# Another order for the first loads and a re-made issue list in a one-core SSM convolution and gated feed-forward kernel

## The chip, the cores and the metric

The kernel runs on one core of a Trainium2 chip. The metric is the device time of one execution in microseconds (us), as the median of several runs. Before the change it is 196.39 us (three runs, 195.62 to 196.74).

## What is computed

The reference, cut to what matters (S = 2048 rows, D = 512, feed-forward width 1792, all bf16):

```python
xn = layernorm(A_q)
# A: shift convolution (4 taps) of k, times v, then a long convolution over the 2048 rows
k_shift = sum_t k_pad[t:t+S] * shift_k[:, ks-1-t]
kv = k_shift * v
y  = irfft(rfft(kv_pad) * rfft(ssm_k_pad))[:S] + kv * ssm_D
s  = xn * y
# B: gated feed-forward
g  = silu((gelu_tanh(xn @ w_gate) * (xn @ w_up)) @ w_down)
out = A_q + s * g
```

## The kernel before

**The work.** The feed-forward runs in four quarters q of 512 rows. For each quarter `ln(q)` (L821 to L835) normalizes four row tiles of 128 (statistics and scaling on VectorE, DVE; the power on GpSimd, POOL), and the tiles are turned with the feature on the partitions: quarters 0 and 1 by transposes on TensorE (PE, L854) and copies into `xnT`, quarters 2 and 3 by a DMA. `unit(q, m)` makes slice m of 14 (128 of the 1792 columns): a gate product and an up product on PE, four matmuls of 512 columns each; ScalarE (ACT) puts the gate through a gelu into `GE` (L1137); DVE multiplies the up product by it into `HT` (L1140). Slices 0 and 1 of quarter 0 are made in two halves of 256 columns (L1128, L1130), the first half from row tiles 0 and 1, the second from tiles 2 and 3. `down(q)` multiplies `HT` by `Wd`. The weights `Wg` and `Wu` come in four pieces each: piece 0 for slices 0 and 1, piece 1 for slices 2 to 5, piece 2 for 6 to 9, piece 3 for 10 to 13.

The long convolution is a Fourier transform in two stages through three scratch tensors in HBM (`ZH`, `ZK`, `ZI`). The filter `ssm_k` arrives as four pieces `Hn` 0 to 3. Pieces 0 and 1 are turned on PE (L878) and evicted as `HTr`. Pieces 2 and 3 are reordered on ACT into `HP` (four copies called HP below, 128x1024 elements, through `copy`, L609: two from piece 2, two from piece 3) and turned by two DMA transposes into `HTD` (L899). `stage1_h` multiplies `HTr` (tasks H) and `HTD` (tasks J) by the Fourier matrix `F1` on PE, ACT evicts, a DMA stores to `ZH`; the J tasks share four buffers, each free again when its store has landed. `stage1_k` does the same for k times v (tasks K). `h_stage2`, `spectrum` and the loop over `psy` do the second stage, the product and the inverse.

**What sets the order.** Nothing is ordered by the loops. `Sched.add` collects some 790 tasks; the string `SEQ` lists them by number, and `Sched.run` goes through `SEQ` in that order, gives each task an engine and takes a buffer or PSUM bank for it by a cost model of its own; then all tasks are emitted in that order. So each engine's instructions stand in the order of `SEQ` and run strictly in it, and a product waits until the earlier user of its PSUM bank, fixed by the list, has been evicted. The costs in the model only choose buffers and banks; the waits are real semaphores. An HP copy stands in the model with `act(1024, True)`, a gelu of 512 columns with `act(512)`; `act(n, sb)` is 170 + 0.833 n, and 30 more for a source in SBUF, in ns.

`ORDER` numbers the input loads; they are issued by SyncE (SP) in the order of `SEQ`, and the DMA transposes and the stores of J and K stand in the same SP queue. A DMA transpose that waits holds up all that stands behind it on SP. The transposes `MI` (two) and `G1` (L1039) share one semaphore, so each waits until the one before has landed. `LANDS` are the model's landing times of the first loads, in ns.

Eleven warm-up matmuls (L618 on a zero tile) stand first on PE. The last thing on PE is the last tile of `down(3)`, followed by silu on ACT (L1172), two DVE steps (L1174, L1175) and the store.

Of the kernel before, what the change touches and what calls it, by code (L numbers as in the profile page):

```python
# [22 lines left out]
LAST = [(0, 384), (384, 512)]  # L23
TURN = 8192
N_WARM = 11
ORDER = "x01 h0 x11 h1 x22 w0 w1 h2 h3 D0 w2 s0 k0 v0 x1 w3 k1 v1 d0 d1 k2 v2 k3 v3 x2 x3"
SEQ = (
# [22 lines left out]
)  # L50
NF_BANKS = 4
ISSUE = 470.0
# [239 lines left out]
class Sched:  # L292
# [8 lines left out]
    FIRST = {"loads": 1050.0, "SP": 30500.0}  # L301
    DRAIN = 121.0
    EARLY, TAKEN, SHARED, WAIT = (0.0, 1.0), 1400.0, 46000.0, 3300.0
    LANDS = (3150.0, 3490.0, 5770.0)

    def __init__(self):
        self.tasks = []
# [37 lines left out]
    def run(self):  # L345
# [5 lines left out]
        for name in SEQ.split():  # L351
# [13 lines left out]
            if eng == "loads":  # L365
                free[eng] = t.start + dur * (self.EARLY[1] if t.start < self.EARLY[0] else 1.0)
                if n_loads < len(self.LANDS):
                    free[eng] = self.LANDS[n_loads] - self.LOAD_LAT
                n_loads += 1
# [29 lines left out]
def build_kernel(nc, A_q, A_k, A_v, A_shift_k, A_ssm_k, A_ssm_D, B_w_gate, B_w_up, B_w_down, out):  # L399
    with ExitStack() as es0:  # L400
# [408 lines left out]

        for what in ORDER.split():  # L810
            if what[0] in "xa" and len(what) == 3:
# [475 lines left out]
```

## Time and profile before

| | |
|---|---|
| median of the runs shown | 196.39 us |
| time of the profiled execution | 195.77 us |
| its span | 194.0 us |
| PE busy in the span | 187.5 us (97%) |
| DVE / ACT / POOL busy | 159.8 / 125.5 / 14.0 us |
| DMA traffic | 49.19 MB, mean 254 GB/s |
| clock granted to PE | full in all slices |

Times in the profile count from the start of the span; the profiled execution took 1.77 us more than its span. A line of the timeline has start, duration, engine, source line, operation, output and inputs, count, and in brackets the idle time before it with what ended it. "x4" merges four instructions; the matmuls are pipelined, so four take less than four times one. SPq and ACTq are DMA issues; "us to landing" runs from the issue to the semaphore.

### The profile page before, as it was taken

Reading aid. Unit: us, or ns where it says so; the run is one execution under the profiler, and the core shown is the slowest. Engines: PE = TensorE matmul, PEld = TensorE weight load, DVE = VectorE, ACT = ScalarE, POOL = GpSimd, SP = SyncE. Lnnn points to the kernel's source line nnn. Section 1 sums busy time; section 2 is a strip of 40 time slices with the busy share of each in tenths; the row PEclk is TensorE's granted clock in tenths of the full one; section 3 lists DMA queues with packets and bytes.
Section 4 is the critical chain, followed back from the end, with each engine's and each line's share of the span. In section 5 each row is a group of like instructions: output and inputs, shape, how many; then the busy total and the mean of one; then the engine's idle time right before and its main releaser. Section 6 shows DMA issues by size and latency. Waiting matters only on the chain.

```text
span 194.0 us, 3492 instructions
## 1 busy us (share of the span) xinstructions
PE 187.5 (97%) x1364; PEld 85.0 (44%) x1377; DVE 159.8 (82%) x245; ACT 125.5 (65%) x170; POOL 14.0 (7%) x32
## 2 busy tenths in 40 slices
PE   7799999999998999999999999999999999999993
PEld 2594544444443444443434433433444434444442
DVE  7599699998999993977788789878897963588993
ACT  6787999979876978868648767756577531222121
POOL 6412420000000000020300000000000000000000
PEclk9999999999999999999999999999999999999999
DMA  5999999999999859999999991893714344939333
GB/s 165 327 322 349 377 403 315 188 217 375 368 363 355 242 210 231 384 345 283 277 306 221 318 312 41 291 332 106 237 37 184 105 150 135 402 109 363 126 139 135
DMA packets 46102, 49.19 MB, mean 254 GB/s; under 512 B 12803, under 2 KB 39943, under 8 KB 46086
## 3 DMA queue, kind: packets, MB, share of 16 engines
q1 hardware_dynamic: 37510, 42.67, 69.8%
q10 hardware_dynamic: 8576, 6.29, 10.1%
q8 instruction: 11, 0.18, 0.4%
q14 instruction: 5, 0.04, 0.1%
HBM read 27.39 MB, written 14.68 MB: 217 GB/s over the span
## 4 chain that ended last, share of the span: by engine, by line
PE 87%; DMA 7%; ACT 2%; issue 1%; SPq 1%; DVE 1%
PE psall L618 80%; PE psall L1028 5%; DMA Hn<-in_A_ssm_k_dram 3%; DMA ZH<-X 3%; SPq L590 1%; PE psall L854 1%; ACT G L609 1%; PE psall L878 1%; ACT X L609 1%; ACT ASX L609 0%; ACT GE L1137 0%; DVE G L1175 0%; DVE G L1174 0%; ACT G L1172 0%
## 5 line engine op out<-in xcount | busy, mean ns | idle before, releaser
L618 PE MATMUL psall<-xnT,Wu 128*128 128x512 bf16 (+1 forms) x232 | 55.8, 372 | 0.0
L618 PE MATMUL psall<-xnT,Wg 128*128 128x512 bf16 (+1 forms) x232 | 55.3, 372 | 0.0
L618 PE MATMUL psall<-Wd,HT 128*128 128x512 bf16 (+2 forms) x231 | 50.8, 366 | 0.7 <-issue 0.5
L1140 DVE TENSOR_TENSOR HT<-psall,GE 128x512 bf16<-128x512 f32 x54 | 36.7, 685 | 15.2 <-PE psall L618 13.6
L1137 ACT ACTIVATE GE<-psall 128x512 bf16<-128x512 f32 x54 | 31.7, 601 | 12.6 <-PE psall L618 12.2
L618 PEld LDWEIGHTS psall<-Wd,HT 128*128 128x128 bf16 x238 | 22.4, 98 | 25.9 <-issue 1.1
L618 PEld LDWEIGHTS psall<-xnT,Wu 128*128 128x128 bf16 x232 | 21.6, 98 | 25.9 <-issue 3.8
L618 PEld LDWEIGHTS psall<-xnT,Wg 128*128 128x128 bf16 x232 | 21.9, 98 | 25.3 <-issue 1.3
L609 ACT ACTIVATE X<-psall 128x1024 bf16<-128x1024 f32 (+1 forms) x18 | 15.1, 846 | 3.8 <-DMA ZH<-X 3.3
L609 ACT ACTIVATE HS<-psall 128x1024 bf16<-128x1024 f32 x14 | 13.7, 1022 | 4.2 <-PE psall L1028 4.2
L1164 ACT ACTIVATE G<-psall 128x512 bf16<-128x512 f32 x12 | 7.0, 597 | 12.8 <-PE psall L618 12.4
L1011 DVE TENSOR_TENSOR KAC<-KAC,KTM 128x2048 bf16<-128x2048 bf16 x12 | 14.6, 1218 | 0.1
L1009 DVE TENSOR_TENSOR KTM<-KK,SKB 128x2048 bf16<-128x2048 bf16 x12 | 14.6, 1217 | 0.0
L609 ACT ACTIVATE BO<-psall 128x1024 bf16<-128x1024 f32 x9 | 9.1, 1023 | 8.2 <-PE psall L1028 7.7
L821 DVE BATCH_NORM_STATS2 stats<-X 128x6 f32<-128x512 bf16 x16 | 10.3, 677 | 3.9 <-DMA X<-in_A_q_dram 3.9
L609 ACT ACTIVATE KB<-psall 128x1024 bf16<-128x1024 f32 x11 | 11.0, 1021 | 3.6 <-PE psall L1028 3.6
L609 ACT ACTIVATE AST<-psall 128x1024 bf16<-128x1024 f32 x12 | 12.3, 1031 | 1.2 <-PE psall L618 1.0
L612 DVE CAST BO<-psall 128x1024 bf16<-128x1024 f32 x7 | 8.5, 1223 | 3.7 <-PE psall L1028 3.7
L1172 ACT ACTIVATE G<-psall 128x512 bf16<-128x512 f32 (+2 forms) x5 | 2.6, 512 | 13.1 <-PE psall L618 13.1
L1091 DVE TENSOR_TENSOR HW<-KB,HW 128x1024 bf16<-128x1024 bf16 x16 | 10.9, 682 | 0.0
L1091 DVE TENSOR_TENSOR HS<-KB,HS 128x1024 bf16<-128x1024 bf16 x16 | 10.8, 682 | 0.0
L618 PE MATMUL psall<-V,F 128*128 128x512 bf16 x30 | 8.8, 379 | 0.4 <-ACT ASX L609 0.3
(83 smaller groups left out, 172.2 us busy)
## 6 DMA issues: line engine op xcount, KB each, us to landing
BH<-ZH SPq DMA_DIRECT2D x8, 512.0 KB, 6.3
HW<-HS SPq DMA_DIRECT2D x16, 256.0 KB, 2.9
BK<-ZK SPq DMA_DIRECT2D x8, 512.0 KB, 5.1
ZI<-BO ACTq DMA_DIRECT2D x16, 256.0 KB, 2.9
BI<-ZI SPq DMA_DIRECT2D x8, 512.0 KB, 4.1
ZK<-AST SPq DMA_DIRECT2D x6, 512.0 KB, 3.7
Hn<-in_A_ssm_k_dram SPq DMA_DIRECT2D x4, 512.0 KB, 8.4
KK<-in_A_k_dram SPq DMA_DIRECT2D x4, 512.0 KB, 8.8
```

The lines of the kernel that those rows point to most:

```text
L609: return h.activation(o, i, ACTF.Copy, scale=scale)
L612: return h.tensor_copy(o, i)
L618: return h.matmul(o, lhsT=l, rhs=r, start=st, stop=sp)
L821: t_stats[t] = op([("DVE", 670.0)], lambda e, h, t=t: h.bn_stats(stats[:, t, :], X[:, t, :]), r=[bX[q][t % 4]], w=[bst[t]], rr=[R_X[t]], w ...
L1009: op([("DVE", dur)], lambda e, h, j=j, m=m: h.tensor_tensor(KTM[:, m.slot, :, :], kk(j), sk(j), ALU.mult), r=need + [bSKB[j], a], w=[m], r ...
L1011: op([("DVE", dur)], lambda e, h, m=m: h.tensor_tensor(KAC[:, a.slot, :, :], KAC[:, a.slot, :, :], KTM[:, m.slot, :, :], ALU.add), r=[m], ...
L1028: trk.op("PE", lambda h: h.matmul(ps(s, i)[b, :], lhsT=wt(col)[a, :], rhs=data(col)[a, :], start=n < 16, stop=n >= len(todo) - 16, tile_po ...
L1091: return hd.tensor_tensor(o, flat(KB, kb[h]), o, ALU.mult)
L1137: op([("ACT", act(512))], lambda e, h: h.activation(GE[:, g.slot, :], bank(pg), ACTF.Gelu_apprx_tanh), r=[pg], w=[g], rr=lambda: R_bank(pg ...
L1140: op([("DVE", dve(512, 1))], lambda e, h: h.tensor_tensor(HT[:, q % 2, m, :], bank(pu), GE[:, g.slot, :], ALU.mult), r=[pu, g], w=[bHT[q][m]],
L1164: op([("ACT", act(n))], lambda e, h, g=g, pc=pc: h.activation(g, pc(), ACTF.Tanh, scale=0.5), r=[p], w=[bt], rr=lambda p=p: R_bank(p), ww= ...
L1172: op([("ACT", act(n))], lambda e, h, g=g, pc=pc: h.activation(g, pc(), ACTF.Silu), r=[p], w=[bt], rr=lambda p=p: R_bank(p), ww=rg, after=z ...
```

## The change

```diff
-ORDER = "x01 h0 x11 h1 x22 w0 w1 h2 h3 D0 w2 s0 k0 v0 x1 w3 k1 v1 d0 d1 k2 v2 k3 v3 x2 x3"
+ORDER = "x02 h0 h1 x22 w0 w1 h2 h3 D0 w2 s0 k0 v0 x1 w3 k1 v1 d0 d1 k2 v2 k3 v3 x2 x3"
 SEQ = (
-    "17 19 18 0 3 1 2 4 8 5 7 11 21 6 9 51 12 66 67 68 74 20 69 76 75 50 10 77 13 53 22 83 23 84 87 118 70 108 71 72 113 55 73 88 78 79 54 370 52 "
+    "0 1 3 17 18 5 11 7 8 9 19 4 2 12 67 50 49 68 6 10 20 65 66 13 75 76 52b 83 73 117 74 87b 118 112 82 86 113 53 102 54 21 369 69 22 70 56 77 "
...
-    LANDS = (3150.0, 3490.0, 5770.0)
+    LANDS = (4350.0, 5700.0, 7000.0, 8420.0, 9400.0, 10250.0)
```

All of `SEQ` differs in its text, since the first row load is one task now and later numbers shift by one. Read by tasks, the following differs.

The loads on SP (KB): before, row tile 0 (128), tile 1 (128), Hn 0 (512), tiles 2 and 3 (256), Hn 1 (512), Wg and Wu piece 0 (256 each), rows of quarter 1 (512), Wg 1 (512), first rows of k (336), D (1), Wu 1 (512), Hn 2, more of k (45), Wg 2, the taps SKR, one row of zeros, k 0, Wu 2, Wg 3, Wu 3, Hn 3 (512 each), then v. After: tiles 0 and 1 in one transfer (256), Hn 0, Hn 1, tiles 2 and 3, Wg 0, Wu 0, Wg 1, rows of quarter 1, Wu 1, first rows of k, SKR, Hn 2, more of k, Wg 2, k 0, Wu 2, zeros, Hn 3, Wg 3, k 1, Wu 3, D, the first HTD transpose, two pieces of v, the second HTD transpose, then the rest.

The start of PE: up to the first gate product both lists hold the same groups (turning Hn 0 and 1, row tiles 0 and 1, six small H products). After it, before: slices 0 and 1 complete (both halves), then slices 3, 5, 2, 4. After: the first halves of 0 and 1, then slices 4, 2, 3 and the ups of 2 and 3, with the second halves between them up to slices 9 and 8.

The four HP copies on ACT: before, `HP, H, gelu 3, gelu 4, H, store, gelu 7, HP, H, gelu 6, 2 xnT, gelu 8, store, gelu 9, xnT, HP, xnT, gelu 11, store, H, HP, gelu 13`. After: `gelu 0 (second half), HP, store, gelu 9, HP, store, HP, gelu 8, HP, xnT, gelu 7, xnT, 2 stores, H, gelu 13`; the third HP is the first that reads Hn 3.

PE at that place, after: gate 0 (second half), up 4, gate 9, up 0 (second half), gate 8, one H product, the transposes of a row tile, up 9, gate 7, up 8, the transposes of another tile, gate 10, up 7, gate 13, transposes, gate 12, gate 6. Gate 10 takes the bank of gate 8, gate 13 the bank of those first transposes, gate 12 that of gate 7.

In the stage of J: after, `MI` from TFB and `G1` stand on SP ahead of the rows of quarter 2 and of the first J store, where before one `MI` stands ahead of them and `G1` comes seven stores later. The rest is small moves; the last products on PE are the same.

42 rows, old and new, of the table SEQ are left out of this document.

## The prediction

> **What bounds the kernel now.** I read the page first, then the chain of waits in order of time, then PE's own waits.
>
> ```profile
> span 194.0 us, 3492 instructions
> PE 187.5 (97%) x1364; PEld 85.0 (44%) x1377; DVE 159.8 (82%) x245; ACT 125.5 (65%) x170; POOL 14.0 (7%) x32
> ```
> ```profile
> 2.59 6.77 DMA Hn<-in_A_ssm_k_dram
> ...
> 9.40 1.17 PE psall L878 x8
> ...
> 159.07 11.82 PE psall L618 x54
> ...
> 190.23 0.02 issue
> ```
> ```profile
> PE psall L878 <- DMA Hn<-in_A_ssm_k_dram: 0.8, 2, 0.6
> PE psall L618 <- ACT ASX L609: 0.3, 1, 0.3
> PE psall L618 <- ACT X L609: 0.2, 1, 0.2
> ```
>
> The chain is a load up to 9.40 us and then nearly all PE until 190.23. From 159.07 on PE makes 54 matmuls of 512 columns in 11.82 us, 0.219 each, with nothing between them; I count 256 columns as half of that and 128 as a quarter. After 9.40 PE waits for other engines only 0.3 + 0.2 us. So the change can win little: some waiting before 9.40, and these 0.5 us. It loses wherever it makes PE wait, because PE has no idle time later in which to catch up.
>
> **First part: the loads and the start of PE.** The rows of the timeline for this part and the next, in order of time, one later HP, and the landing of the first Wg piece (size, us from issue):
>
> ```profile
> 3.06 0.43 SPq L590 DMA_DIRECT2D Wg<-in_B_w_gate_dram  x1
> ...
> 6.04 1.27 PE L878 MATMUL psall<-ident,Hn 128*128 128x128 f32 x8 [0.19 <-DMA Hn<-in_A_ssm_k_dram]
> ...
> 7.99 0.69 DVE L821 BATCH_NORM_STATS2 stats<-X 128x6 f32<-128x512 bf16 x1 [1.27 <-DMA X<-in_A_q_dram]
> ...
> 10.41 0.60 PE L618 MATMUL psall<-xnT,Wg 128*128 128x256 bf16 x4
> ...
> 10.84 0.40 DVE L835 TENSOR_SCALAR XN<-X,mv 128x512 bf16<-128x512 bf16 x1
> ...
> 11.04 0.38 ACT L1128 ACTIVATE GE<-psall 128x256 bf16<-128x256 f32 x1 [0.73 <-PE psall L618]
> ...
> 19.01 2.08 ACT L609 ACTIVATE HP<-Hn 128x1024 bf16<-128x1024 bf16 x1 [0.62 <-DMA Hn<-in_A_ssm_k_dram]
> ...
> 21.00 0.57 ACT L609 ACTIVATE X<-psall 128x512 bf16<-128x512 f32 x1
> ...
> 21.48 0.58 ACT L1137 ACTIVATE GE<-psall 128x512 bf16<-128x512 f32 x1
> ...
> 21.95 0.60 ACT L1137 ACTIVATE GE<-psall 128x512 bf16<-128x512 f32 x1
> ```
> ```profile
> 30.11 2.09 ACT L609 ACTIVATE HP<-Hn 128x1024 bf16<-128x1024 bf16 x1 [0.21 <-DMA Hn<-in_A_ssm_k_dram]
> ```
> ```profile
> Wg<-in_B_w_gate_dram SPq DMA_DIRECT2D x1, 256.0 KB, 7.2
> ```
>
> *Won.* Wg 0 lands at 3.06 + 7.2 = 10.26, and PE starts the first gate product at 10.41. After, the same KB and one issue fewer (0.43 us) stand ahead of it, so it lands between 9.8 and 10.26; I take 10.0, near the middle, and start PE there. The same groups stand on PE up to this point, and Hn 1, for which PE waits now (9.40), moves ahead of tiles 2 and 3, so PE is done with them by then: 0.4 us won. Tiles 0 and 1 in one transfer come some tenths later; PE turns Hn 0 first (6.04), so it does not see that.
>
> *Given back.* Tiles 2 and 3 take the place of Hn 1, which landed at 2.59 + 6.77 = 9.36; less 0.3 for the issue saved, 9.1. From the start of their statistics to the second normalized tile it takes 10.84 + 0.40 − 7.99 = 3.25 us, so that is ready at 12.35. Transposes, the ACT copy and the handing over (about 1.0, an estimate: a gelu's 0.58, four quarter matmuls and PE's 0.2 to be seen, below) put the first product on Wg 1 at 13.4. Behind the first gate's start at 10.0 there is work of 13 matmuls of 512 columns (half of slices 0 and 1, eight transposes, six H products), 2.85 us, so PE could have been there at 12.85: 0.55 lost.
>
> *Other loads.* Hn 2 landed at 19.0 as the 4432nd KB of the list and Hn 3 at 30.1 as the 8061st (two rows wait for them): 327 KB per us. By that rate, less 0.3, Wg 1 (2560 KB) comes at 13.0, Wu 1 (3584) at 16.1, Wg 2 (5501) at 22.0, Wu 2 (6525) at 25.1; PE asks at 13.4, 16.0, 22.15 and 25.05 by the count of its products. All are on the edge, none costs over 0.1.
>
> Sum: 0.55 lost, 0.4 won, **+0.2**. The ends: −0.45 (Wg 0 at 9.8, tiles early enough not to wait) and +0.9 (Wu 1 0.7 later than the rate says).
>
> **Second part: the four HP copies.** This decides.
>
> ```profile
> L609 ACT ACTIVATE HP<-Hn x4: 2082/2084/2107, 19.0 to 34.0; 128x1024 bf16<-128x1024 bf16 x4
> ```
> ```profile
> L609 ACT ACTIVATE HS<-psall 128x1024 bf16<-128x1024 f32 x14 | 13.7, 1022 | 4.2 <-PE psall L1028 4.2
> ```
>
> An HP takes twice as long as an eviction of as many elements (1022 ns), and keeps ACT for 21.00 − 19.01 = 1.99 us; a gelu keeps it for 21.95 − 21.48 = 0.47. The list was made with 170 + 0.833 × 1024 + 30 = 1053 ns for an HP, half of that. Before, the four are spread over 19.0 to 34.0 and enough evictions lie between them. After, the second-half gelu of slice 0, HP, gelu 9, HP, HP, gelu 8, HP and an xnT copy follow each other. Counted from the end of that half's gate on PE:
>
> - ACT sees it after 0.2 (10.41 + 4 × 0.11 = 10.85, the gelu at 11.04). Gelu 0, half the data, 0.3; HP 1.99; gelu 9 0.47; HP 1.99; HP 1.99. Gelu 8 starts at 6.94 and ends, at 0.6, at 7.54.
> - PE goes through up 4, gate 9, half of up 0, gate 8, H, transposes, up 9, gate 7, up 8, transposes: 26 full, 4 half and 8 quarter matmuls, 30 × 0.219 = 6.57. Gate 10 needs the bank that gelu 8 frees: it waits **1.0**.
> - ACT's last HP starts at 7.41 and the xnT copy runs from 9.40 to 9.98. PE, after gate 10 and up 7 (8 × 0.219), stands at 9.3 and needs that bank for gate 13: it waits **0.7**.
> - From there gelu 7 and the next follow 0.5 us apart and stay ahead of PE.
>
> The third HP also needs Hn 3. By the rate it comes as the 7040th KB at 19.0 + 2608 / 327 − 0.3 = 26.7. The half's gate ends near 21.3 on PE, so ACT asks at 21.3 + 0.2 + 0.3 + 1.99 + 0.47 + 1.99 = 26.25: **+0.4**, between 0 and 1.0. Sum **+2.1**, between +1.4 and +3.0; below that only if an HP got shorter in its new place.
>
> [...]
>
> **Third part: the stage of J and K on SP.**
>
> ```profile
> 44.16 6.98 SPq L1039 DMA_TRANSPOSE MI<-TFA  x1
> ...
> 54.98 3.38 SPq L1039 DMA_TRANSPOSE MI<-TFB  x1
> ```
> ```profile
> ACT X L609 <- DMA ZH<-X: 3.3, 3, 1.5
> ```
>
> ACT waits 3.3 us for J stores now, and 0.5 of it reaches PE. After, one `MI` and `G1`, which waits for it, stand ahead of the first J store. Held up 3.38 us like the second `MI`, the store comes about when PE, 2 us later than now, needs it: 0. Held up 6.98 like the first, it is 3.6 us later and 2 to 3 of these reach PE. The v, k and Wd loads that crowd the first `MI` now go out earlier against it, so I take **0**, between −0.5 and +3.
>
> Costed at nothing: v stands behind the first HTD transpose on SP, which waits for the third HP; K wants v some 10 us later. D's late fold and DVE's new order hide behind the waits above; a DVE step that came too late would cost PE up to that step. The last products and what follows them hold the same work.
>
> **Sum.** +0.2 + 2.1 + 0 = +2.3 us. On the profiled execution, span 194.0 and 1.77 around it, 195.77, that makes 198.1; the median lies 0.62 above that execution, and on it the forecast is 196.39 + 2.3 = **198.7 us**. About 0.5% (1.0 us) is what a measurement of this kernel can tell from no change.
>
> **The rivals.**
> - *No difference.* An HP in its new place takes what HS takes; gelu 8 then ends three times 1.0 us earlier, at 4.6, before PE asks at 6.57, and the start is left: 196.39 + 0.2 = 196.6. For it: PE waits for no eviction of this kind now. Against it: four rows within 1% of 2.09. [...] With what else may soften the term, 0.17.
> - *Faster.* One mechanism: the loads land at their early end, PE starts at 9.95 and meets no wait (−0.45), and the 0.5 us of waits on J go: 195.4. It decides at gate 10: gelu 8 must end by 6.5, so an HP may take (6.5 − 1.57) / 3 = 1.6 us. It takes 2.08. 0.05.
> - *The J stores as well.* `MI` holds SP for 7 us again: 198.7 + 2.3 = 201.0. For it: the row of 6.98. Against it: fewer loads beside it. 0.20.
> - *That the change does not do what it says* is excluded for the order; that the loads land no earlier is in the first term.
>
> **How the numbers follow.** The forecast has 0.58; its own range is 196.39 − 0.45 + 1.4 = 197.3 to 196.39 + 0.9 + 3.0 = 200.3. Faster by over 0.5%: 0.05. Within 0.5%: the second case and a little of the forecast's lower edge, 0.18. Slower: 0.77. The range leaves out the faster case, half of the case without a difference and the far half of the J case's: 196.6 to 201.0.
>
> **What would show it.** Right: PE waiting about 1 and 0.7 us for a gelu and an xnT copy between 28 and 33 us; four HP of 2.08 within 11 us; the first gate near 10.0; the last PE work near 192.5. Wrong: PE without a wait from 28 to 33; an HP near 1 us; Hn 3 after 27.3; or PE waiting over 1 us behind J stores or somewhere that I took for covered.

## The result

The changed kernel takes **202.61 us** in the median (201.64 to 203.44, six runs); the kernel before, beside it, 196.77. The ratio is 1.0297, with a 95% interval from 1.0249 to 1.0345: slower by 5.8 us. The forecast of 198.7 had the direction and 2.3 us of it, and the time lies 1.6 us beyond the upper end of the range.

The page of the changed kernel's profile, the line of the span, that of the engines and the granted clock of PE in 40 slices:

```profile
span 199.8 us, 3514 instructions
PE 190.5 (95%) x1377; PEld 84.8 (42%) x1377; DVE 160.2 (80%) x245; ACT 125.7 (63%) x170; POOL 13.1 (7%) x32
...
PEclk9999999999998799999999999999999999999999
```

The span grew by 5.8 us, the busy time of PE by only 3.0, though the work is the same; the clock row is no longer full: in slices 13 and 14, that is from 60 to 70 us, it falls to 0.8 and 0.7. PE's waits, and below them the chain of waits between 45 and 65 us (start, duration, what):

```profile
PE psall L618 <- ACT G L609: 3.3, 1, 3.3
...
PE psall L618 <- ACT GE L1137: 0.9, 1, 0.9
PE psall L618 <- ACT xnT L609: 0.5, 1, 0.5
```
```profile
46.95 8.32 DMA MI<-TFB
...
55.30 1.17 SPq L1039
...
57.13 5.45 DMA ZH<-G
```

Three places can be told apart. The two waits of 0.9 and 0.5 are the two that the prediction set at gates 10 and 13. The longest, 3.3 us, is new: the chain leads back from an eviction of a J task on ACT to the landing of the first J store, from there over SP (rows of quarter 2, `G1`) to the landing of `MI`. This is that place on SP, on ACT and on PE, and then stretches of 2 us, with the busy times of the five engines and behind them the granted clock of PE (0.95 in the first):

```profile
46.95 3.52 SPq L1039 DMA_TRANSPOSE MI<-TFB  x1
55.30 1.17 SPq L1039 DMA_TRANSPOSE G<-F  x1
56.59 0.50 SPq L590 DMA_DIRECT2D X<-in_A_q_dram  x1
57.13 0.43 SPq L590 DMA_DIRECT2D ZH<-G  x1
```
```profile
62.67 1.02 ACT L609 ACTIVATE G<-psall 128x1024 bf16<-128x1024 f32 x1 [5.91 <-DMA ZH<-G]
```
```profile
63.75 1.03 PE L618 MATMUL psall<-V,F 128*128 128x512 bf16 x2 [3.35 <-ACT G L609]
65.16 1.03 PE L618 MATMUL psall<-HTD,F 128*128 128x512 bf16 x2 [0.37 <-ACT X L609]
...
70.04 2.32 PE L618 MATMUL psall<-Wd,HT 128*128 128x512 bf16 x10
```
```profile
62.00:64.00 2.00, 0.25 (x1) 0.13 (x2) 1.82 (x2) 1.33 (x2) 0.00 (x0) 0.95 1.53 305
64.00:66.00 2.00, 1.63 (x5) 0.30 (x4) 0.00 (x0) 1.10 (x2) 0.00 (x0) 0.50 0.86 152
66.00:68.00 2.00, 2.00 (x8) 0.83 (x7) 0.34 (x1) 1.77 (x3) 0.00 (x0) 0.70 1.08 391
```

SP issues `MI` until 50.47 and then nothing until 55.30: `G1` shares its semaphore and waits until `MI` has landed (46.95 + 8.32 = 55.27). Only then come the rows and the first J store, which lands at 57.13 + 5.45 = 62.58. The fifth J task that ACT evicts needs that buffer (there are four), and ACT waits 5.91 us with it; PE waits for the bank behind it, and after 3.35 us of idling it is granted half its clock (0.50 from 64 to 66 us, 0.70 over 66 to 68) until about 67 us. From the end of the wait to the ten matmuls on `Wd` it takes 70.04 − 63.75 = 6.29 us.

The four HP copies on ACT, with the gelu of gate 8 and the xnT copy that PE waited for, and the two gates:

```profile
20.56 2.08 ACT L609 ACTIVATE HP<-Hn 128x1024 bf16<-128x1024 bf16 x1
...
23.01 2.08 ACT L609 ACTIVATE HP<-Hn 128x1024 bf16<-128x1024 bf16 x1
25.23 2.08 ACT L609 ACTIVATE HP<-Hn 128x1024 bf16<-128x1024 bf16 x1 [0.15 <-DMA Hn<-in_A_ssm_k_dram]
...
27.21 0.59 ACT L1137 ACTIVATE GE<-psall 128x512 bf16<-128x512 f32 x1
...
27.69 2.08 ACT L609 ACTIVATE HP<-Hn 128x1024 bf16<-128x1024 bf16 x1
29.66 0.59 ACT L609 ACTIVATE xnT<-psall 128x512 bf16<-128x512 bf16 x1
```
```profile
27.86 1.04 PE L618 MATMUL psall<-xnT,Wg 128*128 128x512 bf16 x4 [0.90 <-ACT GE L1137]
30.31 1.04 PE L618 MATMUL psall<-xnT,Wg 128*128 128x512 bf16 x4 [0.55 <-ACT xnT L609]
```

**Theory A**, formed from these lines: about 4.7 of the 5.8 us come from `G1` waiting on SP ahead of the J stores (3.35 + 0.37 of waits, and some 1.5 of slow products, an estimate from about 3 us of them at half the clock, less the 0.5 that the kernel before waits there); the HP copies cost their 1.5 where they stand, but most of that is hidden, since PE would only wait longer at the J stores. **Rival B**: the bulk loads and `MI` itself make the stores late, whoever waits for whom. **Rival C**: the products behind the wait are slow for another cause than the idling.

### The profile page after: what moved, and what is told of

The parts are those of the page before. It is cut to its first block, busy times and chain, and to the rows that moved or that the text cites. A ratio compares the mean times of both kernels' runs of the same rounds, so it can differ in the third digit from the quotient of the medians.

```text
span 199.8 us, 3514 instructions
## 1 busy us (share of the span) xinstructions
PE 190.5 (95%) x1377; PEld 84.8 (42%) x1377; DVE 160.2 (80%) x245; ACT 125.7 (63%) x170; POOL 13.1 (7%) x32
## 3 DMA queue, kind: packets, MB, share of 16 engines
q10 hardware_dynamic: 8576, 6.29, 9.8%
## 4 chain that ended last, share of the span: by engine, by line
PE 79%; DMA 13%; ACT 2%; issue 2%; SPq 1%; DVE 1%; ACTq 0%
PE psall L618 72%; DMA Hn<-in_A_ssm_k_dram 6%; PE psall L1028 5%; DMA MI<-TFB 4%; DMA ZH<-G 3%; ACT HP L609 1%; PE psall L878 1%; SPq L590 1%; SPq L1039 1%; ACT GE L1137 1%; ACT X L609 0%; PE psall L854 0%; DVE HTr L612 0%; DVE G L1175 0%; DVE G L1174 0%
## 5 line engine op out<-in xcount | busy, mean ns | idle before, releaser
L618 PE MATMUL psall<-Wd,HT 128*128 128x512 bf16 (+2 forms) x238 | 52.9, 367 | 0.0
L1137 ACT ACTIVATE GE<-psall 128x512 bf16<-128x512 f32 x54 | 31.2, 604 | 16.1 <-PE psall L618 12.4
L618 PEld LDWEIGHTS psall<-xnT,Wu 128*128 128x128 bf16 x232 | 22.2, 99 | 25.5 <-issue 2.4
L609 ACT ACTIVATE HS<-psall 128x1024 bf16<-128x1024 f32 x13 | 12.9, 1025 | 4.3 <-PE psall L1028 4.3
L609 ACT ACTIVATE KB<-psall 128x1024 bf16<-128x1024 f32 x12 | 12.0, 1022 | 5.6 <-PE psall L1028 5.5
L609 ACT ACTIVATE X<-psall 128x512 bf16<-128x512 f32 (+1 forms) x16 | 13.0, 823 | 2.7 <-PE psall L618 2.6
L609 ACT ACTIVATE BO<-psall 128x1024 bf16<-128x1024 f32 x10 | 9.9, 1022 | 5.5 <-PE psall L1028 5.4
L618 PE MATMUL psall<-V,F 128*128 128x512 bf16 x32 | 9.8, 394 | 3.3 <-ACT G L609 3.3
L1166 DVE SCALAR_TENSOR_TENSOR G<-G,psall 128x512 bf16<-128x512 bf16 x12 | 8.0, 681 | 5.4 <-ACT G L1164 5.4
L612 DVE CAST BO<-psall 128x1024 bf16<-128x1024 f32 x6 | 7.3, 1224 | 5.8 <-PE psall L1028 5.8
```

Source lines behind the costliest of these rows:

```text
L609: return h.activation(o, i, ACTF.Copy, scale=scale)
L612: return h.tensor_copy(o, i)
L618: return h.matmul(o, lhsT=l, rhs=r, start=st, stop=sp)
L1137: op([("ACT", act(512))], lambda e, h: h.activation(GE[:, g.slot, :], bank(pg), ACTF.Gelu_apprx_tanh), r=[pg], w=[g], rr=lambda: R_bank(pg ...
L1166: op([("DVE", dve(512, 1))], lambda e, h, g=g, pc=pc: h.scalar_tensor_tensor(out=g, in0=g, scalar=1.0, in1=pc(), op0=ALU.add, op1=ALU.mult ...
```

## The experiments

Times of one row come from one chip with runs of the kernel before beside them, so rows are compared by the ratio.

| kernel | median, us | before beside it | ratio, 95% interval |
|---|---|---|---|
| the changed kernel | 202.61 | 196.77 | 1.0297 [1.0249, 1.0345] |
| G1, MI: a semaphore each | 197.76 | 195.92 | 1.009 [1.0056, 1.0124] |
| J 0 eight times | 200.9 | 195.92 | 1.0267 [1.0193, 1.034] |
| HP in address order | 203.45 | 195.92 | 1.0378 [1.031, 1.0445] |
| semaphores, HP in address order | 196.63 | 195.92 | 1.0028 [0.9992, 1.0064] |
| first loads alone | 196.69 | 196.21 | 1.0042 [1.001, 1.0074] |
| G1 alone moved | 197.0 | 196.21 | 1.0041 [1.0019, 1.0062] |
| semaphores, HP apart | 197.27 | 196.21 | 1.0059 [1.0026, 1.0093] |
| the same, MI and G1 behind | 196.78 | 196.21 | 1.0028 [1.0003, 1.0053] |
| HP in address order, J 0 thirteen times | 201.35 | 195.75 | 1.0268 [1.0224, 1.0312] |
| MI and G1 behind as above, HP on POOL | 199.5 | 195.75 | 1.0198 [1.0165, 1.023] |
| before, MI and G1 behind | 195.84 | 195.75 | 1.0009 [0.9979, 1.0038] |

### G1 no longer waits for MI

```diff
-        d_g1 = dsem("d_g1")
+        d_g1 = [dsem(f"d_g1_{i}") for i in range(3)]
-  ... transpose=True), d_g1, r=[rr], w=[ww])
+  ... transpose=True), d_g1[0 if ww is R_G1 else 1 if ww is R_MI[0] else 2], r=[rr], w=[ww])
```

> The changed kernel with one edit: the transposes G1 and MI have a semaphore each, so G1 no longer waits on SP for the landing of the MI ahead of it; the order of the list is the same. Theory A (what SP loses from 50.5 to 55.3 us behind that landing makes the J stores, ACT's eviction of J 5 and so PE late): G1 issues within 1 us of the end of MI's issue, the first J store 3.5 to 5 us earlier, ACT waits under 2.5 us for it instead of 5.9, PE's wait of 3.35 us goes or falls under 0.7, its clock stays full from 62 to 68, and the time is 198.0 us (197.4 to 199.0), 4 to 5 below the changed kernel. Rival B (the queues are full with bulk loads, and the store comes late by these whoever waits for whom): the first store still lands at 61 us or later, and the time falls by under 1 us.

SP and PE in the profile of this kernel:

```profile
47.55 3.52 SPq L1039 DMA_TRANSPOSE MI<-TFB  x1
51.11 1.26 SPq L1039 DMA_TRANSPOSE G<-F  x1
52.49 0.51 SPq L590 DMA_DIRECT2D X<-in_A_q_dram  x1
54.16 0.38 SPq L590 DMA_DIRECT2D ZH<-G  x1
```
```profile
61.06 0.59 PE L618 MATMUL psall<-V,F 128*128 128x512 bf16 x2
```

`MI` is issued at the same place with the same 3.52 us, `G1` right behind it, the store 2.97 us earlier than in the changed kernel, and PE starts the K product without a wait (no bracket). 1.0297 − 1.009 is 2.1% or 4.1 us. So `MI`'s own issue is not what costs, and rival B is out as far as these 4.1 us go. The store did not come 3.5 us earlier, as expected: SP now waits at 53 us for ACT, the store's data being what is last.

### G1 alone moved

The three transposes share their semaphore again; only `G1` is emitted later on SP, behind the store of K 3, with buffers and banks as they were.

```diff
 MI<-TFB
-G<-F
 X<-in_A_q_dram
...
 ZK<-AST
+G<-F
 X<-in_A_q_dram
```

> The changed kernel with one task moved: G1 issues on SP behind the eighth store after the second MI instead of right behind the first MI; all three transposes still share their semaphore. Theory A (G1 standing ahead of the stores, in wait for MI, is what costs): the first J store issues at 53 to 55 us, PE waits under 1 us there, and the time is that of the kernel with the separate semaphores, 197.0 to 198.5 us. Rival B (the semaphore as such, whoever waits on it, or the transposes' traffic): the second MI now waits in its place and the time stays within 1.5 us of the changed kernel's.

The first store issues at 54.24, and PE has no wait there. 1.0297 − 1.0041 is 2.6%, 5.0 us: the small move of one short transpose in the list is worth nearly the whole loss. The second `MI` still shares the semaphore, and issues at 56.56, when the first has landed anyway; it matters where the waiting task stands, not that there is a semaphore.

### PE kept busy during the wait

```diff
-                    for c in range(2):
+                    for c in [0, 1] * (8 if x == "J" and u == 0 else 1):
```

> The changed kernel with one edit: the two matmuls of task J 0, which stand on PE 1.7 us ahead of the wait of 3.35 us, are made eight times over (14 matmuls of 512 columns, about 3.07 us, with the same result), so that PE works where it was idle. Nothing else moves. Theory A (PE's idle time of 3.35 us costs more than itself, because its granted clock falls to one half after it): no wait over 0.6 us at that place, clock 0.9 or more from 62 to 68, and the time falls by 1.2 to 1.9 us although PE has 3 us more work: 200.7 to 201.4. Rival C (the slow products from 64 to 68 are slow for another cause, such as ACT's evictions behind them): the time stays within 0.5 us of the changed kernel or rises.

The K product behind the wait and the ten on `Wd`, and the clock (the same columns as above):

```profile
64.77 0.59 PE L618 MATMUL psall<-V,F 128*128 128x512 bf16 x2
...
69.26 2.32 PE L618 MATMUL psall<-Wd,HT 128*128 128x512 bf16 x10
```
```profile
64.00:66.00 2.00, 2.00 (x10) 0.71 (x9) 1.34 (x2) 1.31 (x2) 0.00 (x0) 1.00 1.24 220
```

The same products take 4.49 us instead of 6.29, at full clock: 1.8 us, of which 0.4 are the second wait. By the time alone (1.0267 against 1.0297) the two kernels can't be told apart. The kernel with thirteen such products, below, repeats this with more at stake.

### HP copies in address order, alone and with the semaphores

```diff
-  Hn[:, 2 + k, :].rearrange("p (a t) -> p t a", t=NT)[:, 8 * hf:8 * hf + 8, :]
+  Hn[:, 2 + k, :].rearrange("p (t a) -> p t a", t=NT)[:, 8 * hf:8 * hf + 8, :]
```

> The changed kernel with one edit: the four HP copies read pieces 2 and 3 of the filter in address order instead of every 16th element; the J half of the filter is therefore wrong and nothing else differs in instructions. Theory A (the stride makes an HP of 2.08 us out of 1.0; the 1.77 us that PE loses at gates 10 and 13 hang on it; but the end of the later J stall is set by SP and the queues, not by PE): HP takes 1.0 to 1.1 us, PE waits under 0.3 us from 26 to 33 us, and yet the time falls by only 0.3 to 1.3 us (201.3 to 202.3), the wait at the J stores being longer by most of what was won. Rival D (the two losses add up): the time falls by 1.7 to 2.2 us, to 200.4 to 200.9. Rival E (stride is not the cause): HP stays at 2.08 us, and the time with it.

> Both edits together: a semaphore each for G1 and MI, and the HP copies read in address order (the J half of the filter is wrong). Theory A: with the J stall out of the way the HP term shows in the end: 1.5 to 2.0 us below the kernel with the semaphores alone, 196.2 us (195.6 to 197.2), as fast as the kernel before or half a us faster. If the HP term is hidden for good, it stays within 0.5 us of the kernel with the semaphores alone.

The group of HP in the first of the two (busy time, mean ns), its wait at the J stores, and its clock from 62 to 74 us:

```profile
L609 ACT ACTIVATE HP<-Hn 128x1024 bf16<-128x1024 bf16 x4 | 4.2, 1050 | 1.1 <-DMA Hn<-in_A_ssm_k_dram 1.1
```
```profile
65.11 1.03 PE L618 MATMUL psall<-V,F 128*128 128x512 bf16 x2 [5.53 <-ACT G L609]
...
72.72 2.32 PE L618 MATMUL psall<-Wd,HT 128*128 128x512 bf16 x10
```
```profile
62.00:66.00 4.00, 0.89 (x2) 0.13 (x2) 1.01 (x1) 1.97 (x3) 0.00 (x0) 0.80 1.21 318
66.00:70.00 4.00, 3.63 (x10) 1.28 (x10) 0.71 (x2) 2.87 (x4) 0.00 (x0) 0.50 1.06 326
70.00:74.00 4.00, 4.00 (x17) 1.66 (x16) 3.97 (x4) 2.06 (x3) 0.00 (x0) 0.85 0.50 182
```

The stride is what makes an HP long: 2.08 us with it, 1.05 without it, and PE has no wait from 25 to 33 us. Yet this kernel is not faster, which was a miss of theory A (0.3 to 1.3 us less were expected). In its profile PE is done ahead of the J stores at 59.6 us instead of 60.4, although it started 0.7 later, but its wait ends at 65.11 instead of 63.75: `MI` is issued at 48.60 and `G1` at 57.00, 1.7 us later than in the changed kernel, for a reason that no run shows. PE idles 5.53 us instead of 3.35 and is then slow for longer (a clock of 0.50 over 66 to 70 us); the stretch that took 6.29 us takes 7.61. So the 1.5 us of the HP copies are hidden, and the longer idling gives back at least as much. With the J stall gone the HP term shows: 1.009 − 1.0028 is 0.6% or 1.2 us of the 1.5, with intervals that overlap at their ends; in the profile PE waits 0.5 and 0.8 us at the J stores, where the rest may have gone.

### The same with PE kept busy

The kernel with HP in address order, and J 0 made thirteen times.

> The kernel with the HP copies read in address order (the J half of the filter is wrong), which was to be faster than the changed kernel and was not: its PE stood idle 5.53 us at the J stores and its clock was at one half for 5 us after that. Here the products of J 0 ahead of that wait are made thirteen times over (24 matmuls more, 5.2 us), so that PE is busy while it would wait. Theory A (what was won at gates 10 and 13 became a longer wait, and the longer wait a longer stretch at half clock): from the first K product behind the wait to the ten matmuls on Wd it takes 4.5 us, as in the kernel with eight such products, instead of 8 or more, and the time falls by 2.5 to 3.5 us to 200.0 to 201.0 us, although PE has 5 us more work. Rival (the loss of that kernel lies elsewhere, for instance in queues that its early HP copies upset): the time stays within 1 us of 203.45.

The K product starts at 66.39 us and the ten on `Wd` at 70.71: 4.32 us instead of 7.61, with 5.2 us more work on PE. 1.0378 − 1.0268 is 1.1% or 2.2 us less, a little under the 2.5 expected, with intervals that just touch. Together with the clock rows this speaks against rival C. The rival of this run is out only in part: `G1` is issued at 56.72 us here, late as in the kernel without the extra products, so some of that kernel's loss may come over SP.

### HP copies apart, and the transposes behind the stores

Both kernels have a semaphore for each transpose and every buffer and bank as in the changed kernel. In the first, the third HP (with its HTD transpose) is emitted behind gelu 8 and the fourth behind gelu 7. In the second, besides, the first `MI` and `G1` behind the sixth store of J and K, the other `MI` behind the twelfth. On ACT in both, and on SP in the second:

```diff
 HP<-Hn
-HP<-Hn
 GE<-psall
 HP<-Hn
 xnT<-psall
 GE<-psall
+HP<-Hn
 xnT<-psall
```
```diff
 KK<-in_A_k_dram
-MI<-TFB
-G<-F
 X<-in_A_q_dram
...
 ZH<-X
-MI<-TFA
 ZH<-G
 ZK<-AST
 ZH<-G
+MI<-TFB
+G<-F
 ZK<-AST
...
 ZK<-AST
+MI<-TFA
 X<-in_A_q_dram
```

> The changed kernel with separate semaphores for G1 and MI, and the four HP copies apart on ACT: gelu 0, HP, gelu 9, HP, gelu 8, HP, xnT copy, gelu 7, HP (each HTD transpose behind its two copies); all results, buffers and banks as in the changed kernel. Theory A (gates 10 and 13 wait for what stands behind the HP copies, not for anything of their own): no wait of PE over 0.4 us from 26 to 33 us with HP at 2.08 as before; as in the kernel with short HP copies, up to 1.3 us of the 1.5 won there is lost again to the J stores, so 196.6 us (196.0 to 197.4). If nothing is lost again: 196.2. If HTD, which comes 0.3 to 1 us later, is on the path: 197.5 or more.

> The kernel of the run before this one, and besides the first MI and G1 moved behind the sixth store of J and K on SP, the second MI behind the tenth, so that no transpose stands ahead of the first J store. Theory A (what is left to wait for at the J stores is their own landing, slowed by the transposes' traffic beside them): stores land in 3 to 5 us instead of 5 to 6, PE waits under 0.5 us from 56 to 66 us, and the time is 195.5 us (194.8 to 196.3), below the kernel before by 0.3 to 1.3 us. Rival: the transposes hold up the later stores instead, and the time is that of the run before this one or above.

PE's waits up to 70 us in the first, and in the second:

```profile
10.65 1.05 PE L618 MATMUL psall<-xnT,Wg 128*128 128x256 bf16 x8 [1.58 <-DMA Wg<-in_B_w_gate_dram]
23.81 1.02 PE L618 MATMUL psall<-xnT,Wg 128*128 128x512 bf16 x4 [0.74 <-DMA Wg<-in_B_w_gate_dram]
30.05 1.02 PE L618 MATMUL psall<-xnT,Wg 128*128 128x512 bf16 x4 [0.45 <-DMA Wg<-in_B_w_gate_dram]
62.78 0.60 PE L618 MATMUL psall<-HTD,F 128*128 128x512 bf16 x2 [0.49 <-ACT X L609]
```
```profile
9.83 1.05 PE L618 MATMUL psall<-xnT,Wg 128*128 128x256 bf16 x8 [0.35 <-DMA Wg<-in_B_w_gate_dram]
16.31 1.02 PE L618 MATMUL psall<-xnT,Wu 128*128 128x512 bf16 x4 [0.26 <-DMA Wu<-in_B_w_up_dram]
32.46 1.04 PE L618 MATMUL psall<-xnT,Wg 128*128 128x512 bf16 x4 [0.37 <-ACT xnT L609]
```

The waits for gelu 8 go in both, and in the second those at the J stores; one of 0.37 us for an xnT copy behind the fourth HP stays. What shows besides are weights that land late. The waits up to 23.81 us stand ahead of the first copy that was moved, so the edit did not make them. The first took 197.27, inside the expected range though above its 196.6, with 0.45 us of wait for `Wg` where none was expected. The second has no wait at the J stores, as expected, and yet missed its 195.5 by 1.3 us: it can't be told from the first, and it is still 0.3% slower than before. What these 0.3% are stays open; the first loads, next, would suffice, but no run takes them out of this kernel.

### The first loads alone

The kernel before with the changed order of the first loads (tiles 0 and 1 at once, `Hn` 0, `Hn` 1, tiles 2 and 3, `Wg` 0, `Wu` 0), everything else as it was.

```diff
-ORDER = "x01 h0 x11 h1 x22 w0 w1 h2 ...
+ORDER = "x02 h0 h1 x22 w0 w1 h2 ...
```

> The kernel before with one part of the change alone: row tiles 0 and 1 in one transfer, then both filter pieces, then tiles 2 and 3, then the weights; the rest of its list and all buffers and banks stay. Theory A (the new first loads land earlier than the prediction had it and cost nothing at tiles 2 and 3): the first gate at 9.0 to 9.8 us instead of 10.41, PE 0.4 to 0.9 us ahead from there on, and 0.3 to 0.9 us faster than before at the end, as the kernel before has only 0.5 us of waits at the J stores in which it could be lost. The prediction's first term (tiles 2 and 3 late, 0.55 lost and 0.4 won): within 0.3 us of before.

DVE's first work on tile 2, and PE's waits (the lines of this kernel's file stand one further down):

```profile
8.99 0.69 DVE L822 BATCH_NORM_STATS2 stats<-X 128x6 f32<-128x512 bf16 x1 [2.07 <-DMA X<-in_A_q_dram]
```
```profile
10.03 0.60 PE L619 MATMUL psall<-xnT,Wg 128*128 128x256 bf16 x4 [1.04 <-DMA Wg<-in_B_w_gate_dram]
11.37 0.40 PE L855 MATMUL psall<-ident,XN 128*128 128x128 bf16 x4 [0.74 <-DVE XN L836]
```

Tiles 2 and 3 land at 9.0, and PE waits 0.74 us for them: the loss that the prediction described (9.1 and 0.55). The new first loads gain nothing by themselves, they cost 0.4%, which is 0.8 us (0.2 to 1.5); theory A's expectation here was wrong. It had been read off one profile. The 0.3 us expected by the prediction's first term were too little as well.

### HP on POOL, and the transposes moved in the kernel before

Two attempts at a kernel that beats both. The first is the kernel with the transposes behind the stores, with the four HP tasks on POOL. The second is the kernel before with three semaphores, one `MI` moved behind the stores on SP, the other and `G1` behind the store of K 2 (its order on SP is the second diff).

```diff
+    for t in order:
+        if t.n in (57, 58, 59, 60):
+            t.eng = "POOL"
```
```diff
 Wd<-in_B_w_down_dram
-MI<-TFA
 KK<-in_A_k_dram
...
 ZH<-X
-MI<-TFB
 ZK<-AST
 ZH<-X x2
 ZH<-G
-G<-F
+MI<-TFA
 ZH<-G
...
 ZK<-AST
+MI<-TFB
+G<-F
 BH<-ZH x2
```

> The kernel with separate semaphores and all transposes behind the first J stores, with the four HP copies on POOL instead of ACT (POOL is idle from 23.4 us on; its copies of 512 elements of the taps take 0.91 us each there, so about 1.8 us an HP, two of them between 23.5 and 27, the other two behind them to 31). Theory A (HP on ACT is what is left of the second term): no wait of PE for ACT from 26 to 36 us, and 0.5 to 0.9 us less than the kernel with HP on ACT: 196.0 us (195.4 to 196.6), level with the kernel before or up to 0.5% below it. Rival (POOL's copies slow DVE's work beside them, or HTD comes too late for the J products at 52 us): 196.8 us or more.

> The kernel before with the edit that helped the changed one: a semaphore each for MI and G1, the first MI behind the sixth J store, the second and G1 behind the store of K 2. Theory A: PE's waits for J stores (0.3 + 0.2 us) go and nothing else moves: 0.3 to 0.6 us faster than before, just short of what can be told or just at it. Rival (the transposes are needed earlier than thought, or disturb what now stands beside them): no change or slower.

HP on POOL, DVE's work on k beside it and after it, and PE's longest wait for DVE (us in all, times, the longest):

```profile
L612 POOL COPY HP<-Hn 128x1024 bf16<-128x1024 bf16 x4 | 10.1, 2542 | 0.1
```
```profile
28.84 2.46 DVE L1009 TENSOR_TENSOR KTM<-KK,SKB 128x2048 bf16<-128x2048 bf16 x1
31.23 0.68 DVE L1140 TENSOR_TENSOR HT<-psall,GE 128x512 bf16<-128x512 f32 x1
31.83 2.45 DVE L1011 TENSOR_TENSOR KAC<-KAC,KTM 128x2048 bf16<-128x2048 bf16 x1
...
34.80 1.21 DVE L1009 TENSOR_TENSOR KTM<-KK,SKB 128x2048 bf16<-128x2048 bf16 x1
```
```profile
PE psall L854 <- DVE HT L1140: 1.2, 2, 0.8
```

On POOL an HP takes 2.54 us, 0.7 more than was worked out from the copies of the taps, and the three steps of DVE on k (both inputs in SBUF) that start before it is done take 2.15 to 2.46 us, where they take 1.21 to 1.22 with HP on ACT. PE waits 1.2 us for DVE at `HT` and 0.45 at `XN`, later also 0.5 and 0.8 us for ACT at 40 and 49 us, and the kernel is 1.7% (3.3 us) slower than with HP on ACT; that those later waits come from DVE too is not shown. The second attempt changed nothing that can be told (0.9979 to 1.0038), and PE's waits of 0.3 and 0.2 us at the J stores, which were to go, are still there: the `MI` ahead of the stores did not make them. So no version here beats the kernel before.

## Why the prediction was right or wrong, point by point

**The third part failed.** The prediction put the stage of J and K at 0, "between −0.5 and +3"; it is 4 to 5 us (the two kernels without `G1`'s wait). Two things were wrong in its working. It said that `G1` waits for `MI`, and then held the store up by `MI`'s issue, 3.38 or 6.98 us as in the rows of before; what holds up SP is `MI`'s landing, 8.32 us from its issue, because a task that waits for it stands directly behind. In the kernel before, four stores stood on SP between the second `MI` and `G1`. Its profile had the number that was wanted, the us from issue to landing:

```profile
MI<-TFA SPq DMA_TRANSPOSE x1, 10.8
MI<-TFB SPq DMA_TRANSPOSE x1, 6.2
```

Second, it counted idle time of PE as its own length only: 3.35 us of idling cost about 1.4 us more in slow products (6.29 us against 4.49 with PE kept busy, less the second wait of 0.37). The rival "The J stores as well" (201.0, 0.20) names the right place with half the price. Its mechanism, `MI` holding SP for 7 us by its issue, is not what happened: `MI` was issued in 3.52 us, and the wait for its landing held SP.

**The second part was right where it stands.** Forecast: four HP of 2.08 us within 11 us, PE waiting 1.0 us for gelu 8 at gate 10 and 0.7 for the xnT copy at gate 13. Seen: four of 2.08 from 20.56 to 29.77, 0.90 and 0.55. The third copy waited 0.15 for `Hn` 3, where 0.4 was counted. What the sum missed is that the terms don't add: as long as the J stall ends at a time set by SP, these 1.5 us come out of that stall, and the kernel with short HP copies is no faster. With the stall gone they are worth about 1.2 us.

**The first part** (+0.2, between −0.45 and +0.9) holds as far as can be told: by themselves, in the kernel before, the new first loads cost 0.8 us (0.2 to 1.5), and the start scatters in a way that the prediction did not know. The first gate on PE stands at 9.03 us in the profile of the changed kernel, against 10.41 before and 10.0 forecast. But nine other profiles with the same start have it at 9.27, 9.55, 9.64, 9.75, 9.83, 9.87, 9.90, 10.15 and 10.65, and the kernel before with the transposes moved, whose start is that of before, at 9.36. No difference between the two starts can be read from that. The steps under it were sound: tiles 2 and 3 land at 9.0 where 9.1 was worked out, in the run with the loads alone.

**The rivals.** "No difference" fell with HP at 2.08. "Faster" needed an HP under 1.6 us at gate 10; with 1.05 us and `G1` out of the way it comes to level with before, not below it.

**The sum by the runs:** 4.1 to 5.0 us for `G1` at the J stores with the slow clock behind it; about 1.2 for HP once that stall is gone; about 0.8 for the first loads in the kernel before, which no run isolates in the changed one. They add up to 6.1 to 7.0 against the 5.8 measured, and each of them is uncertain by about 1 us. The forecast of 2.3 lacked the first of them.

## What to carry to other kernels

When a task that waits for a semaphore moves in a queue, price the landing that it waits for, not the issue of the transfer ahead of it (8.32 us against 3.52 here), and list every store behind it with the buffer that the store frees. Where an engine waits twice, a gain at the first wait is lost at the second if that one's end is set by another queue, as the 1.5 us of the HP copies were here: take the later wait away first. And read a start or a landing from several profiles before giving it a sign; the one profile here was 0.8 us off the median of its own kind.

## What the runs showed of the hardware

- **PE's granted clock after two idle times.** After 3.35 us idle, 0.50 from 64 to 66 us; full again from about 67.2 (0.70 over 66 to 68 is 1.2 us at one half), some 3.5 us after it resumed. With PE kept busy at that place, 1.00 from 62 to 68. After 5.53 us idle, at one half from about 64.4 (0.80 over 62 to 66), while PE still stood idle, until about 71.2 by the same reckoning, 6 us after it resumed. In the second case the return took longer; another idle gap of 0.37 us lies in both, so it does not explain this, and the cause stays open.
- **HP on ACT, with and without its stride.** 128x1024 bf16 with every 16th element read: 2.08 us; in address order 1.05. HP was run with no other stride.
- **POOL beside DVE.** While POOL copied HP (2.54 us each), DVE's steps on k, with both inputs in SBUF, took 2.15 to 2.46 us instead of 1.21, and those on `HT`, with an input in PSUM, stayed at 0.68. Three `XN` steps took 3.42 us in all, against 1.73 with HP on ACT. No run shows the cause.
- **One DMA transpose's landing in two places.** The same `MI` from TFB lands 8.3 us after its issue at 46.95 us, behind the loads of k and `Wd`, and 4.7 us after it when issued at 60.60 behind the stores; `G1` takes 2.3 us in the changed kernel and 4.9 in the one with a semaphore each. What the transfers beside them do to this was not separated.
